# A fused attention and two-layer expert kernel: the region of fixed emission order is taken out and the framework's scheduler orders every engine

## The chip, the cores and the metric

The kernel runs on one core of a Trainium2 chip. The metric is device time in microseconds of one execution, as the median of several runs. A core has five engines that run side by side, each with a queue of its own in a fixed order: TensorE (PE in the profile, with its weight loads shown as PEld), VectorE (DVE), ScalarE (ACT), GpSimd (POOL) and SyncE (SP), which here only issues transfers. Transfers run on 16 DMA engines.

## The reference, cut to what matters

```python
scores = q @ k.T / sqrt(64)              # 4 batches, 8 heads, 576 positions, head size 64
scores = where(block_i >= block_j, scores, -1e9)      # blocks of 64 positions
attn = exp(scores - max); attn /= sum(attn) + 1e-9
x = (attn @ v) as 2304 tokens x 512
x2 = (sigmoid(x @ w_gate) * (x @ w_val)) @ w_out      # 512 -> 1536 -> 512
e = argmax(x2 @ r_gate); p = softmax(x2 @ r_gate)[e]  # one of 8 experts for each token
out = p * (relu(x2 @ w1[e]) @ w2[e])                  # 512 -> 1024 -> 512
```

## The kernel before

All of it is one Python function, `attn_moe_moe_kernel` (L25 to L1322), whose inner functions emit instructions. The body from L1072 on stands in a region of fixed emission order:

```python
    with tc.manual_schedule():          # L1072
        ag = attention()
        ...
        for n, (kind, u, f) in enumerate(msegs):       # L1121: unit u, 128 columns f
            if kind == "g":
                while wdone[0] < count(t_in(f)):
                    next(wg)
                m_gate(u, f)
            elif kind == "v":
                m_val(u, f)
                if f < KF - 1 or not DEFER:
                    m_act(u, f)
```

In such a region every engine issues its instructions in the order in which the Python code emits them. That order is written out by hand, as strings of letters: in `Q0` to `Q4` (L94), `G0` to `H4` (L99) and `TICK0` to `TICK2` (L87, L112), each letter emits one step and a bar separates segments. Semaphores between the engines are the framework's in any case.

The work goes through four stages.

- **Attention of the first batch** (`quick`, L411). A pair is two heads of a batch; an item is 128 query rows of a pair, five items to a pair, 80 in all. An item's steps are S (scores on PE, L253 for the first batch, L262 and L269 later), M (row maximum on DVE, L290 or L292), E (exp on ACT, L306), r and c (reciprocal of the sum on DVE, L323, L325), N (normalizing, L360 on DVE or L358 on ACT), T and U (transposes on PE, L337, copied out by ACT, L339), V (times v on PE, L382) and X (two halves of the result on ACT and DVE, L390, L391, stored by a GpSimd transfer, L393). K and Q (`prep`, L211) transpose the next pair's k and q (L216). Two items are under way at a time.
- **Conversion of the weights** (`weights`, L595). The three matrices of the first layer come as 64-bit numbers, are rounded to 32 bits and split in a high and a low part: two ACT operations (L569, L588) and four DVE operations (L570, L574, L579, L590) for each piece of 128x1024. The letter d and a pacing counter (`pace`) step this generator between the steps of the attention, later between those of the first unit. `w_load` (L550) issues a piece's transfer, 1 MB, into one of four buffers as soon as the code knows that the buffer has been read.
- **The first layer** (units u = 0 to 8 of 256 tokens, 12 column blocks f each). `m_gate` and `m_val` do 12 matmuls each (L633 to L635), `m_act` the sigmoid and the product on ACT and DVE (L654 to L658), `m_out` the second product (L670). The first six units or so are interleaved with the attention of batches 2 to 4: a credit counter calls `seg()`, which emits the attention up to the next bar. In the last unit the routing (`route_early`, small DVE operations) and the first expert's splits (`early_split`) are stepped in between, and `x_trans(0)` (L1007) transposes the first gathered rows behind `m_val` of f = 10.
- **The experts** (`tick`, L1236, 20 slots of 128 tokens). Each slot has `gemm1` and `gemm2` in halves (L1021), `h_trans` and `x_trans` (PE transposes, an ACT copy, and a DVE subtraction, L1044 and L1010), and four splits of the next expert's weights, each an ACT cast (L974) and a DVE subtraction (L975), after which SP loads the weights of the slot after next. `TICK1` is "AxB0amy1CD2b3": A and C are the halves of `gemm1`, B and D those of `gemm2`, a and b the transposes of h, x that of the next slot's rows, 0 to 3 the splits.

Buffers are few: the scores have one PSUM buffer in the later stages, transposes and attention outputs share two (`ea`), gate and value products two (`gv`), exp results two, k and q one each.

Of the kernel before, what the change touches and what calls it, by code (L numbers as in the profile page):

```python
# [24 lines left out]
def attn_moe_moe_kernel(  # L25
# [1043 lines left out]
        )  # L1069


    with tc.manual_schedule():  # L1072
        ag = attention()
        done = [-3]

# [277 lines left out]
```

## Time and profile before

| what | value |
|---|---|
| median of 3 runs | 1022.13 us (1018.63 to 1022.52) |
| the profiled execution | 1020.07 us, of which 1018.3 us lie between the first and the last instruction |
| busy: PE, DVE, ACT, POOL | 945.5, 619.3, 588.0, 122.6 us |
| mean granted clock of PE | 0.986 |

Busy times are read as sums over the whole span: matmuls overlap one another, so PE at 100% of a stretch may still have no more than its instructions in a row. A row of stretches gives, for each stretch, the busy time of each engine, the granted clock as a share of full speed, the mean share of the DMA engines and the rate in GB/s.

### The profile page before, as it was taken

To read this page: it belongs to the slowest core of one execution; us is meant where nothing else is said; L and a number is where in the kernel's file an instruction comes from. 1 tells how busy PE (TensorE), PEld (TensorE's weight loads), DVE (VectorE), ACT (ScalarE), POOL (GpSimd) and SP (SyncE) were. 2 spreads that over 40 slices of the span, in tenths; PEclk is the share of its full clock that TensorE was granted. 3 is DMA by queue.
4 is the path that set the end of the run, shared out by engine and by line. 5 is a ranking of instruction groups with operands and counts; after the bars stand their busy time and mean duration, and the time that the engine had idled before them with its cause. 6 is when DMAs were issued, how large, how long until landed. Compare 5 with 4: busy or idle time off the path is not lost. (4 is left out here: it accounts for less than half of the span.)

```text
span 1018.3 us, 17756 instructions
## 1 busy us (share of the span) xinstructions
PE 945.5 (93%) x6636; PEld 809.0 (79%) x6636; DVE 619.3 (61%) x1178; ACT 588.0 (58%) x1204; POOL 122.6 (12%) x169
## 2 busy tenths in 40 slices
PE   6767887999999999999999999999979999999994
PEld 3444776888888888988888889999968888888883
DVE  5997876545445445445444321122749999888985
ACT  5877555655544554555545321212358878888884
POOL 1111000111001000010010100000022223112110
PEclk9898999999999999999999999999999999999998
DMA  9965240511221131131130110101551552969110
GB/s 253 278 191 178 72 120 26 138 44 41 76 65 41 56 84 36 58 82 42 46 81 14 46 41 1 63 1 63 189 169 57 209 170 82 375 228 340 47 42 20
DMA packets 111161, 106.07 MB, mean 104 GB/s; under 512 B 62175, under 2 KB 83679, under 8 KB 111072
## 3 DMA queue, kind: packets, MB, share of 16 engines
q1 hardware_dynamic: 104128, 84.97, 27.1%
q0 software_dynamic: 6944, 19.93, 5.9%
q8 instruction: 54, 0.88, 0.4%
q14 instruction: 35, 0.29, 0.1%
HBM read 140.53 MB, written 19.40 MB: 157 GB/s over the span
## 5 line engine op out<-in xcount | busy, mean ns | idle before, releaser
L633 PE MATMUL gv<-xu,w 128*128 128x256 f32 x864 | 253.5, 293 | 0.8 <-ACT et L339 0.8
L635 PE MATMUL gv<-xu,w 128*128 128x256 f32 x864 | 244.3, 283 | 1.6 <-DVE w L590 1.6
L634 PE MATMUL gv<-xu,w 128*128 128x256 f32 x864 | 244.2, 283 | 0.0
L975 DVE TENSOR_TENSOR el<-raw,eh 128x2048 fp32r<-128x2048 f32 x84 | 191.7, 2290 | 27.0 <-ACT eh L974 25.8
L670 PE MATMUL acc<-w,g 128*128 128x512 f32 x648 | 184.1, 410 | 3.9 <-ACT g L657 3.9
L633 PEld LDWEIGHTS gv<-xu,w 128*128 128x128 f32 x864 | 165.0, 191 | 7.7 <-issue 5.0
L634 PEld LDWEIGHTS gv<-xu,w 128*128 128x128 f32 x864 | 165.1, 191 | 1.5
L635 PEld LDWEIGHTS gv<-xu,w 128*128 128x128 f32 x864 | 164.7, 191 | 1.8 <-DVE w L590 1.8
L974 ACT CAST eh<-raw 128x2048 fp32r<-128x2048 f32 x84 | 161.0, 1918 | 5.2 <-DMA raw<-in_moe_w_dram 5.1
L655 DVE SCALAR_TENSOR_TENSOR th<-th,gv 128x256 f32<-128x256 f32 x108 | 45.4, 420 | 150.6 <-ACT th L654 150.5
L670 PEld LDWEIGHTS acc<-w,g 128*128 128x128 f32 x648 | 111.5, 190 | 24.2 <-ACT g L657 4.3
L654 ACT ACTIVATE th<-gv 128x256 f32<-128x256 f32 x108 | 41.5, 385 | 133.7 <-PE gv L635 133.5
L393 POOL DMA_DIRECT2D x_d<-x x80 | 55.0, 688 | 494.2 <-DVE x L391 289.8
L1021 PE MATMUL hp<-eh,xt 128*128 128x512 f32 x320 | 109.2, 402 | 0.0
L1021 PE MATMUL yp<-eh,ht 128*128 128x512 f32 x320 | 106.2, 393 | 0.7 <-ACT ht L1043 0.7
L306 ACT ACTIVATE e<-sp,nm 128x128 f32<-128x128 f32 (+3 forms) x128 | 66.5, 526 | 49.9 <-DVE nm L290 47.3
L657 ACT CAST g<-th 128x256 fp32r<-128x256 f32 x108 | 43.9, 406 | 67.5 <-DVE th L655 62.9
L658 DVE TENSOR_TENSOR g<-th,g 128x256 fp32r<-128x256 f32 x108 | 45.9, 425 | 53.3 <-ACT g L657 53.3
L382 PE MATMUL av<-et,v 128*64 128x128 f32 (+1 forms) x960 | 67.7, 273 | 8.0 <-ACT et L339 6.1
L337 PE MATMUL ep<-ident,e 128*128 128x128 f32 x320 | 57.3, 285 | 15.0 <-ACT e L358 5.6
L1021 PEld LDWEIGHTS yp<-eh,ht 128*128 128x128 f32 x320 | 59.9, 188 | 13.6 <-ACT ht L1043 0.9
L1021 PEld LDWEIGHTS hp<-eh,xt 128*128 128x128 f32 x320 | 60.2, 188 | 11.8
(182 smaller groups left out, 1399.6 us busy)
## 6 DMA issues: line engine op xcount, KB each, us to landing
raw<-in_moe_w_dram SPq DMA_DIRECT2D x88, 1024.0 KB
xu<-x_d SPq DMA_DIRECT2D x36, 256.0 KB
x_d<-x POOLq DMA_DIRECT2D x64, 128.0 KB, 2.2
spare<-in_moe_w_gate_dram SPq DMA_DIRECT2D x10, 512.0 KB
spare<-in_moe_w_val_dram SPq DMA_DIRECT2D x10, 512.0 KB
spare<-in_moe_w_out_dram SPq DMA_DIRECT2D x10, 512.0 KB
x_d<-x2r SPq DMA_DIRECT2D x9, 512.0 KB
k<-in_k_dram SPq DMA_DIRECT2D x32, 128.0 KB
```

The source lines that it names most:

```text
L306: nc.scalar.activation(out=r["e"][:, j, 0:n], in_=r["view"][:, j, :], func=AF.Exp, bias=r["nm"][:, j:j + 1], accum_out=su[:, j:j + 1],)
L337: nc.tensor.transpose(ep[:, cs], r["e"][:, part, cs], ident)
L382: nc.tensor.matmul(av[hs, 0:m], lhsT=d["v"][:, c, j, :], rhs=rhs, start=(c == 0), stop=(c == t))
L393: nc.gpsimd.dma_start(out=x_d[hp][:, :, t0:t0 + m], in_=x[:, :, 0:m].bitcast(F32))
L633: nc.tensor.matmul(o, lhsT=wh, rhs=x[:, 0, :], start=(kk == 0 and nm == "g"), stop=False, **kw)
L634: nc.tensor.matmul(o, lhsT=wh, rhs=x[:, 1, :], start=False, stop=False, **kw)
L635: nc.tensor.matmul(o, lhsT=wl, rhs=x[:, 0, :], start=False, stop=(kk == KD - 1), **kw)
L658: nc.vector.tensor_tensor(out=g[:, 1, :], in0=th, in1=g[:, 0, :], op=ALU.subtract)
L670: nc.tensor.matmul(o, lhsT=g[:, part, hs], rhs=w_o(w, f), start=(f == 0 and w == "h" and part == 0), stop=(f == KF - 1 and part == 1),)
L974: nc.scalar.copy(out=h, in_=raw[j])
L975: nc.vector.tensor_tensor(out=l, in0=raw[j], in1=h, op=ALU.subtract)
L1021: nc.tensor.matmul(o, lhsT=t[:, cs], rhs=w[:, c * 512:(c + 1) * 512], start=(first and c == 0 and part == 0 and w is eh), stop=(last and c ...
```

## The change

The region is replaced by an empty context, so the same Python code emits the same instructions with the same buffers in the same sequence, but no engine is held to that sequence.

```diff
@@ -1069,7 +1069,7 @@
         )
 
 
-    with tc.manual_schedule():
+    with ExitStack():
         ag = attention()
         done = [-3]
 
```

The framework then runs its list scheduler when the kernel is built. It walks through the program in a modelled time of its own; whenever an engine is free in it, it takes, among the instructions of that engine whose inputs and buffers are ready by the model, the one emitted first. The outcome is again one fixed order for each engine, which the chip follows as it followed the order by hand.

## Rows read from the trace of the kernel before

**Rows 1.** The page's first lines: span, busy time and instructions of each engine

```profile
span 1018.3 us, 17756 instructions
...
PE 945.5 (93%) x6636; PEld 809.0 (79%) x6636; DVE 619.3 (61%) x1178; ACT 588.0 (58%) x1204; POOL 122.6 (12%) x169
```

**Rows 2.** Busy time in stretches: start:end, length, engines, PE clock, DMA, GB/s

```profile
0.00:25.00 25.00, 16.09 (x82) 8.90 (x82) 14.37 (x32) 14.04 (x35) 2.71 (x10) 1.00 0.94 251
25.00:95.00 70.00, 48.99 (x376) 30.62 (x377) 62.45 (x116) 55.83 (x136) 11.39 (x21) 0.88 0.69 210
95.00:175.00 80.00, 65.77 (x507) 57.94 (x505) 60.20 (x144) 47.66 (x125) 7.27 (x14) 0.98 0.32 93
175.00:225.00 50.00, 48.07 (x383) 41.21 (x384) 27.33 (x74) 27.17 (x80) 5.53 (x12) 1.00 0.31 85
225.00:600.00 375.00, 366.74 (x2953) 326.18 (x2951) 175.77 (x481) 187.95 (x535) 37.36 (x71) 1.00 0.21 56
600.00:740.00 140.00, 140.00 (x1032) 129.18 (x1031) 44.95 (x132) 35.19 (x81) 2.63 (x1) 1.00 0.18 61
740.00:780.00 40.00, 34.68 (x203) 28.82 (x202) 25.02 (x23) 26.82 (x33) 7.77 (x6) 1.00 0.40 126
780.00:1000.00 220.00, 219.76 (x1088) 182.34 (x1087) 202.38 (x178) 188.33 (x179) 46.92 (x36) 1.00 0.50 175
```

**Rows 3.** What PE waited for in 0 to 95 us: total, times, longest

```profile
PE ep L337 <- ACT e L358: 5.6, 5, 1.7
...
PE ep L337 <- DVE e L360: 4.7, 7, 1.0
```

**Rows 4.** DVE's groups in 25 to 95 us: busy us, mean ns, idle before

```profile
L574 DVE SCALAR_TENSOR_TENSOR spare<-spare,spare 128x1024 int32<-128x1024 int32 x10 | 12.2, 1215 | 0.0
L579 DVE CUSTOM_DVE_ANT_0 spare<-spare,spare 128x2048 uint16<-128x2048 uint16 x10 | 12.1, 1213 | 0.0
L590 DVE TENSOR_TENSOR w<-spare,w 128x1024 fp32r<-128x1024 f32 x9 | 11.0, 1218 | 0.0
...
L570 DVE TENSOR_SCALAR spare<-spare 128x1024 int32<-128x1024 int32 x9 | 6.4, 715 | 0.0
L391 DVE TENSOR_TENSOR x<-av,x 128x128 fp32r<-128x128 f32 (+1 forms) x15 | 4.1, 274 | 2.5 <-ACT x L390 2.5
```

**Rows 5.** The order of time in the first 25 us, SP and PE

```profile
9.03 1.17 SPq L186 DMA_DIRECT2D k<-in_k_dram  x2
...
16.63 0.51 SPq L557 DMA_DIRECT2D spare<-in_moe_w_gate_dram  x1
...
19.39 1.12 PE L216 MATMUL tp<-ident,k 128*128 128x128 f32 x5
```

**Rows 6.** One of DVE's groups in 225 to 600 us

```profile
L391 DVE TENSOR_TENSOR x<-av,x 128x128 fp32r<-128x128 f32 (+1 forms) x47 | 12.8, 272 | 25.7 <-ACT x L390 25.5
```

**Rows 7.** What PE waited for in 225 to 600 us: total, times, longest

```profile
PE ep L337 <- ACT et L339: 2.7, 2, 1.4
PE tp L216 <- issue: 2.6, 3, 0.9
PE sp L262 <- ACT x L390: 2.2, 3, 0.8
```

**Rows 8.** The order of time around 742 us, PE

```profile
742.06 0.28 PE L635 MATMUL gv<-xu,w 128*128 128x256 f32 x1
...
745.50 0.66 PE L1007 MATMUL xtp<-ident,xs 128*128 128x128 f32 x4 [3.16 <-DMA xs<-x_d,gi]
...
745.91 0.36 PE L633 MATMUL gv<-xu,w 128*128 128x256 f32 x1
```

**Rows 9.** The order of time in one expert slot, DVE and PE

```profile
857.95 0.69 DVE L1044 TENSOR_TENSOR ht<-htp,ht 128x512 fp32r<-128x512 f32 x1
858.55 2.29 DVE L975 TENSOR_TENSOR el<-raw,eh 128x2048 fp32r<-128x2048 f32 x1
...
859.37 1.07 PE L1021 MATMUL yp<-eh,ht 128*128 128x512 f32 x4
```

## The prediction, made before the changed kernel was run

> **What bounds the kernel now.** I read the page's busy line first. PE is busy for 945.5 of 1018.3 us [rows 1]: it is the engine to look at, and 72.8 us of idle time is all that any order could win from it, because the change adds and removes no instruction.
>
> Then I cut the span into stretches by stage [rows 2], and the reader is to see four regimes. From 0 to 95 us (attention of the first batch, with nine or ten weight pieces converted in between) PE is busy 65.1 of 95 us and DVE 62.5 of the 70 us from 25 on, 89%: DVE is the fullest engine, and PE waits in chains of small steps, most of all for the normalized rows [rows 3]. From 95 to 225 us (first unit, the rest of the conversion) PE lacks 16.2 us while DVE has 19.8 us free from 95 to 175. From 225 to 740 us PE is the bound, idle for 8.3 us of 515. At 740 to 780 us, the passage to the experts, it lacks 5.3 us. From 780 to 1000 us it lacks 0.2 us of 220, but DVE stands at 92% there (202.38 of 220) and ACT at 86%, so the experts are close to a second bound. The last 18 us hold the drain and the end of the program; no order of the work ahead changes them.
>
> So the idle time that could be won is early, and the long stretches that could be lost are full already.
>
> **The change, part by part.** It removes edges of order and nothing else. The scheduler takes the ready instruction that was emitted first. Where the head of the emission order is ready in its model, it repeats the order by hand; it departs from that only where the model says that the head must wait. So each term below is a place where heads wait today, and the trace doesn't show what the model thinks of them: both ends are bounded, and the value is a choice.
>
> *Conversion moved forward, 95 to 225 us.* DVE's 19.8 free microseconds from 95 to 175 [rows 2] hold 4.5 pieces at 4.36 us each (1.215 + 1.213 + 1.218 + 0.715) [rows 4]. If they are used, the first unit's weights come earlier, and PE's 16.2 idle microseconds go at best entirely. At worst nothing is won, since the free time lies in waits on ACT that no piece fits into. I take half: -8 (0 to -16).
>
> *Conversion in front of the attention, 25 to 95 us.* An operation that has begun isn't interrupted. The conversion runs on DVE for 41.7 of the 70 us in 38 operations, 1.10 us each [rows 4]. By hand it stands behind chosen letters; a scheduler that fills every gap starts one whenever the attention's next step is a moment away. An item comes to DVE four times (M, r, N, X); 15 items pass here by the count of L391 [rows 4]. With DVE in a conversion 60% of the time and half an operation, 0.55 us, to wait: 15 x 4 x 0.60 x 0.55 = 19.8 us if nothing covers it, and 0 if the order by hand has paid all of it already, for which PE's 21 idle microseconds there speak. Two items are under way, so I take half: +10 (0 to +20).
>
> *Loads overtaken on SP, 0 to 25 us.* Today SP issues the second pair's k at 9.03 us and the next weight pieces only from 16.63 us on [rows 5]. Pieces two to four have free buffers from the start and may go ahead of k, which waits for its one buffer. Three pieces of 1.05 MB at 251 GB/s [rows 2] are 12.5 us of transfer. Covered is what lies between the issue of k at 9.03 and its use at 19.39 us [rows 5], less its own flight: +2 (0 to +12). SP's later waits are for buffers in either order, and GpSimd, busy for 122.6 us in all [rows 1], has room for its stores: 0.
>
> *Attention between the unit's matmuls, 225 to 600 us.* 48 items pass here (47 in the row's count, where a record may be missing) [rows 6]. PE waited 7.5 us in eight waits, 0.94 us each [rows 7], because a segment of matmuls stands between each producer and PE's next use. The scheduler knows no such margin: it puts the transposes where its model has the rows ready, and a wait appears whenever ACT or DVE is later than modelled. One new wait in every four items gives 12 x 0.94 = +11; one in each item +45; none, and the present ones filled, -8. I take +11, since PE is full and heads are mostly ready.
>
> *Passage to the experts, 740 to 780 us.* PE stands for 3.16 us behind a gathered block while the next unit block's matmuls, which run right after it, wait in line [rows 8]. A scheduler moves these ahead. I take -3 (-5.3, all the idle time, to +2.3, one split of 2.29 us [rows 9] in front of a routing step).
>
> *Splits in the experts, 780 to 1000 us.* In the slot shown, DVE delivers the low half of h at 858.64 (857.95 + 0.69) and PE uses it at 859.37: 0.73 us of margin, and the split right behind takes 2.29 us [rows 9]. If one more split goes in front, PE stands for 2.29 - 0.73 = 1.56 us. There are 20 slots with two such steps. None is lost at best, 40 x 1.56 = 62 us at worst. By the model the low half is ready about when it is today and was emitted before the split, so I take one in ten: 4 x 1.56 = +6.
>
> The sum is -8 + 10 + 2 + 11 - 3 + 6 = +18. The profiled execution took 1020.07 us, 1.8 us over its span of 1018.3 [rows 1]; with +18 it is 1038. It lies 2.1 us under the median of the runs (1022.13), so I forecast 1040 us.
>
> Of the clock: PE's granted clock is 0.88 from 25 to 95 us, a mean of its two levels, 2.4 and 1.2 GHz, and 1.00 where PE is full [rows 2]. The Trainium skill (TensorE: Matmul & The Clock Gate, "What's actually happening") says that the low level is the default and that activity releases it; by that, a fuller PE in this stretch would also run faster. At 0.88 a quarter of PE's 49.0 busy microseconds would be at half speed, about 6 us to win as an estimate from the row. I leave it out of the sum, because DVE and not PE is the fullest there.
>
> **The rivals.**
>
> *The order hardly changes (no difference).* If the heads are ready in the model nearly everywhere, the scheduler repeats the emission order. For it: PE, where all is decided after 225 us, is full, so its heads are ready. Against it: DVE and ACT wait often (DVE 25.5 us in one group alone [rows 6]), so their orders will change. It gives 1022 us, 1017 to 1027.
>
> *The gaps are filled (faster).* The mechanism is the conversion on DVE from 0 to 175 us: it decides if the last piece is converted some 10 us earlier than today with the first batch's attention ending no later than today, about 97 us. Then 12 of the 16.2 idle microseconds go, and 3 at the passage: 1022 - 15 = 1007 us. For it: DVE's free 19.8 us [rows 2]. Against it: DVE is full just before, and the end of the attention depends on steps that wait behind conversions. The Trainium skill (Perfetto Trace Analysis, "Optimization Strategy") says that interleaving regimes with different bounds may improve a kernel; this rival is that rule, and the rows agree that the first 175 us have two regimes.
>
> *The experts and the attention both lose their margins (much slower).* One split in front of one of the two low halves in each slot costs 20 x 1.56 = 31 us, and a wait in every second attention item 24 x 0.94 = 23 us; with +10 and +2 early and no gain: +66, 1088 us. For it: DVE at 92% and a margin of 0.73 us. Against it: the emission order ranks the low half first.
>
> **How the numbers follow.** The forecast's own case (1028 to 1062) has 0.42, much slower 0.20, no difference 0.14, faster 0.24. Half a percent, 5 us, is about what a measurement of this kernel can tell from no change. So slower has 0.62, the same 0.14, faster 0.24. The range goes from 1002, under the faster case, to 1090, over the much slower one; what lies outside is a gain of all the bounds together or a loss near them.
>
> **What would show it.** In the changed profile I would look at the same stretches. Right: PE's first 95 us with more idle time than 29.9 us and the first gate matmul later than now; the last conversion (L590) earlier than now; in 225 to 600 us more and shorter waits of PE on L339 and L360; the gather's wait gone; in the experts waits of PE on L1044. The prediction is wrong if the first 225 us shrink by more than 10 us and the rest stands, or if the experts' stretch grows by tens of microseconds, or if some resource that I have not priced, such as a buffer taken by later work, makes PE stand for long at one place.

## The result, and the profile after

The changed kernel is a little faster: 1018.86 us as the median of 19 runs (1004.75 to 1020.65), against 1023.29 (1018.63 to 1026.48, 19 runs) of the kernel before. The ratio is 0.9912, with a 95% interval of 0.9883 to 0.9941; it is taken from means, without the three runs over 1020 us, which count as slow; with all 19 the means give 0.9922, and the two medians 0.9957. I had forecast 1040 us, slower.

The 19 times lie in two groups, and the groups are those of PE's mean granted clock: nine runs of 1004.75 to 1015.12 us at 0.975 to 0.991, and ten of 1018.86 to 1020.65 us at 0.967 to 0.969. The profile shown here is of a run of the first group: 1009.74 us.

The page's first lines and its row of PE's clock in 40 slices:

```profile
span 1007.8 us, 17820 instructions
...
PE 957.1 (95%) x6636; PEld 811.4 (81%) x6636; DVE 610.5 (61%) x1178; ACT 591.9 (59%) x1204; POOL 127.7 (13%) x169
...
PEclk9997999999999999999999999999999999999998
```

It is the same work as in [rows 1], in a span 10.5 us shorter. The stretches of [rows 2], of the kernel after:

```profile
0.00:25.00 25.00, 11.99 (x46) 6.26 (x46) 12.75 (x26) 9.55 (x24) 1.10 (x8) 1.00 0.84 232
25.00:95.00 70.00, 60.41 (x393) 33.08 (x391) 58.93 (x116) 56.78 (x139) 13.90 (x25) 0.90 0.81 241
95.00:175.00 80.00, 76.13 (x586) 67.13 (x583) 66.97 (x165) 55.23 (x145) 8.15 (x15) 0.96 0.35 97
...
225.00:600.00 375.00, 372.71 (x2992) 331.43 (x2991) 173.65 (x473) 186.63 (x524) 35.33 (x69) 1.00 0.20 54
...
780.00:1000.00 220.00, 209.20 (x1018) 171.60 (x1017) 186.46 (x158) 174.85 (x166) 48.84 (x33) 0.99 0.48 170
```

The first 25 us are emptier than before on PE (16.09 to 11.99), the next 200 fuller [rows 2]. Fixed times no longer mean the same work, though, so I cut both spans again at four events that every run has: the first scores (L253), the first gate matmul (L633), the last second product of the first layer (L670), and the last expert product (L1021). In us:

| stretch | before | after | change |
|---|---|---|---|
| start to the first scores | 8.33 | 15.01 | +6.7 |
| first scores to first gate | 89.16 | 88.46 | -0.7 |
| first gate to last product of the first layer | 658.4 | 635.2 | -23.2 |
| from there to the last expert product | 250.2 | 255.3 | +5.0 |
| from there to the end | 12.2 | 13.9 | +1.7 |

These add up to the -10.5. The gain is in one stretch; three others give back more than half of it. Where in that stretch it lies is seen by windows laid from the first gate on (97.5 us before, 103.5 after), the first two of equal length in both. Before:

```profile
97.50:177.00 79.50, 65.30 (x504) 57.71 (x501) 60.42 (x147) 45.57 (x121) 6.69 (x14) 0.98 0.29 86
177.00:227.50 50.50, 49.34 (x396) 42.48 (x396) 26.04 (x69) 29.11 (x86) 6.18 (x12) 1.00 0.33 89
227.50:585.30 357.80, 349.54 (x2831) 310.03 (x2829) 171.56 (x467) 181.06 (x518) 35.25 (x63) 1.00 0.20 55
585.30:755.90 170.60, 167.44 (x1209) 154.13 (x1210) 53.51 (x152) 45.18 (x100) 7.47 (x11) 1.00 0.22 75
```

After:

```profile
103.50:183.00 79.50, 78.16 (x617) 70.07 (x616) 64.12 (x165) 54.49 (x146) 7.57 (x14) 1.00 0.34 94
183.00:233.50 50.50, 49.77 (x422) 43.21 (x421) 28.58 (x77) 29.59 (x88) 5.35 (x10) 1.00 0.21 50
233.50:569.20 335.70, 333.41 (x2694) 296.27 (x2694) 162.44 (x439) 174.93 (x492) 33.00 (x60) 1.00 0.20 56
569.20:738.70 169.50, 167.71 (x1209) 153.97 (x1210) 53.01 (x152) 46.02 (x99) 6.88 (x11) 1.00 0.23 80
```

In the 79.5 us while the weights are still converted, PE's idle time fell from 14.2 us to 1.3, and it issued 113 matmuls more (617 against 504). In the next 50.5 us it fell from 1.2 us to 0.7, in the rest of the attention's stretch from 8.3 to 2.3, in the last window from 3.2 to 1.8. These are 20.6 of the 23.2 us; the other 2.6 are busy time of PE, whose clock was 0.98 in the first window before and 1.00 after. The conversion's last operation (L590), before and after:

```profile
176.53 0.42 DVE L590 TENSOR_TENSOR w<-wt,w 128x256 fp32r<-128x256 f32 x1
...
156.81 0.43 DVE L590 TENSOR_TENSOR w<-wt,w 128x256 fp32r<-128x256 f32 x1
```

It ends 53.8 us after the first gate, where it had been 79.5. But PE had not waited for weights in the main. Of the 15.4 us of idle time in these first two windows before, 1.6 were a wait for converted weights; most of the others were for steps of the attention and of the unit, which DVE and ACT do too. One of each kind:

```profile
PE acc L670 <- ACT g L657: 3.9, 2, 3.1
...
PE gv L635 <- DVE w L590: 1.6, 1, 1.6
```

What PE waited for afterwards, in 0 to 95 us, for [rows 3]:

```profile
PE tp L216 <- DVE kn L223: 7.5, 1, 7.5
PE ep L337 <- ACT e L358: 4.7, 3, 2.1
PE tp L216 <- DMA k<-in_k_dram: 4.4, 1, 4.4
...
PE ep L337 <- DVE e L360: 0.2, 1, 0.2
```

In 225 to 600 us, for [rows 7], nothing else is left:

```profile
PE tp L216 <- issue: 1.6, 3, 0.5
PE ep L337 <- ACT et L339: 0.6, 2, 0.3
```

And from 740 to 1000 us, where the kernel before had lost 0.9 us in its experts:

```profile
PE yp L1021 <- ACT y L1061: 3.2, 1, 3.2
PE hp L1021 <- ACT xt L1009: 0.8, 1, 0.8
PE yp L1021 <- ACT ht L1043: 0.7, 1, 0.7
PE yp L1021 <- DVE ht L1044: 0.5, 1, 0.5
PE htp L1041 <- ACT h L1032: 0.3, 1, 0.3
```

So the new waits are not where I had looked for them. One wait of 7.5 us stands at the very start; the order of time on ACT, DVE and PE there, after:

```profile
11.78 1.14 ACT L569 ACTIVATE spare<-spare 128x1024 int32<-128x1024 uint32 x1 [5.83 <-DMA spare<-in_moe_w_val_dram]
11.79 0.69 DVE L570 TENSOR_SCALAR spare<-spare 128x1024 int32<-128x1024 int32 x1 [10.53 <-DMA spare<-in_moe_w_val_dram]
12.40 0.75 DVE L223 COPY kn<-tp 128x576 f32<-128x576 f32 x1
...
13.21 1.12 PE L216 MATMUL tp<-ident,q 128*128 128x128 f32 x4 [7.52 <-DVE kn L223]
```

The scheduler put the first conversion on DVE ahead of the copy of the transposed k (L223). On the chip the piece's transfer let it start only at 11.79 us. The copy, whose transposes had run from 4.38 to 5.68 us, stood behind it, and PE's buffer for the q transposes waits for the copy. By hand the copy ran at 5.61 us and these transposes at 6.56.

### The profile page after: what moved, and what is told of

The parts are those of the page before. It is cut to its first block, busy times and chain, and to the rows that moved or that the text cites. A ratio compares the mean times of both kernels' runs of the same rounds, so it can differ in the third digit from the quotient of the medians.

```text
span 1007.8 us, 17820 instructions
## 1 busy us (share of the span) xinstructions
PE 957.1 (95%) x6636; PEld 811.4 (81%) x6636; DVE 610.5 (61%) x1178; ACT 591.9 (59%) x1204; POOL 127.7 (13%) x169
## 5 line engine op out<-in xcount | busy, mean ns | idle before, releaser
L633 PE MATMUL gv<-xu,w 128*128 128x256 f32 x864 | 253.4, 293 | 0.7 <-ACT et L339 0.7
L975 DVE TENSOR_TENSOR el<-raw,eh 128x2048 fp32r<-128x2048 f32 x84 | 191.9, 2288 | 23.2 <-ACT eh L974 21.7
L670 PE MATMUL acc<-w,g 128*128 128x512 f32 x648 | 184.1, 409 | 1.2 <-DVE g L658 1.2
L633 PEld LDWEIGHTS gv<-xu,w 128*128 128x128 f32 x864 | 164.6, 191 | 8.1 <-issue 5.4
L670 PEld LDWEIGHTS acc<-w,g 128*128 128x128 f32 x648 | 110.6, 189 | 21.2 <-issue 3.3
L1021 PE MATMUL yp<-eh,ht 128*128 128x512 f32 x320 | 108.1, 398 | 4.4 <-ACT y L1061 3.2
L1021 PE MATMUL hp<-eh,xt 128*128 128x512 f32 x320 | 109.0, 402 | 0.8 <-ACT xt L1009 0.8
L306 ACT ACTIVATE e<-sp,nm 128x128 f32<-128x128 f32 (+3 forms) x128 | 67.0, 529 | 23.2 <-DVE nm L290 22.4
L1021 PEld LDWEIGHTS yp<-eh,ht 128*128 128x128 f32 x320 | 60.1, 189 | 18.7 <-ACT y L1061 4.1
L339 ACT COPY et<-ep 128x128 f32<-128x128 f32 (+3 forms) x128 | 53.7, 428 | 30.8 <-PE ep L337 29.2
L1021 PEld LDWEIGHTS hp<-eh,xt 128*128 128x128 f32 x320 | 59.9, 188 | 12.8 <-ACT xt L1009 1.3
L382 PEld LDWEIGHTS av<-et,v 128*64 128x64 f32 x960 | 48.1, 139 | 24.0 <-ACT et L339 7.2
```

The costliest lines, as they stand in the source:

```text
L306: nc.scalar.activation(out=r["e"][:, j, 0:n], in_=r["view"][:, j, :], func=AF.Exp, bias=r["nm"][:, j:j + 1], accum_out=su[:, j:j + 1],)
L339: nc.scalar.copy(out=et[:, 0:w], in_=ep[:, 0:w])
L382: nc.tensor.matmul(av[hs, 0:m], lhsT=d["v"][:, c, j, :], rhs=rhs, start=(c == 0), stop=(c == t))
L633: nc.tensor.matmul(o, lhsT=wh, rhs=x[:, 0, :], start=(kk == 0 and nm == "g"), stop=False, **kw)
L670: nc.tensor.matmul(o, lhsT=g[:, part, hs], rhs=w_o(w, f), start=(f == 0 and w == "h" and part == 0), stop=(f == KF - 1 and part == 1),)
L975: nc.vector.tensor_tensor(out=l, in0=raw[j], in1=h, op=ALU.subtract)
```

## The experiments

All of them put `with tc.manual_schedule():` back around parts of the changed kernel; nothing of the computation changes. My theory from the profile above was that the scheduler wins some 23 us between first gate and passage by moving the conversion forward, and loses in the first batch; what Theory 1 and Theory 2 say of each run stands in its expectation. Each ratio is to the kernel before on the same chip, where that kernel's median lay between 1020.77 and 1024.26 us. "Low clock" is the time in the first 130 us at which the trace's record of the clock grants PE 1.2 GHz, added up from windows of one microsecond: 20.5 us before and 20.5 in the profile after.

That record begins late, with its first entry at 20.15 us before and 25.99 us after; ahead of it the windows, those of [rows 2] too, read 1.00. PE's matmuls show that it ran at the low level there: four transposes of 128x128 (L337) took 1.12 us from 23.43 us on in the profile after, and as many took 0.66 from 25.48 us on before, in a stretch that is recorded at 2.4 GHz. So low clock leaves this first stretch out, and where its length differs it is named below.

**The changed kernel once more**, to see how much of a profile repeats (no edit).

> The changed kernel once more, for a profile of an execution of its own. Its 19 times lie in two groups, some 1005 to 1015 us with mean clocks of 0.975 to 0.991 and some 1019 to 1021 us with 0.967 to 0.969. Theory 1 (PE's clock): if the time is near 1019, the extra low clock lies in the first 130 us, and the milestones from there on are later by the same 10 us. Theory 2 (transfers): the clock is then a result, and one long wait on a transfer, longer than in the profile at hand, stands ahead of it. If the time is near 1009, it tells nothing new.

It took 1008.61 us at a clock of 0.984. Low clock 20.5 us, first gate at 102.52 us, 635.2 us from there to the last product of the first layer: the profile repeats.

**First batch by hand.**

```diff
-        while done[0] < NB - 3:
...
+        with tc.manual_schedule():
+            while done[0] < NB - 3:
...
```

> The first batch's attention, with its share of the conversion, keeps the order by hand; units and experts are the scheduler's. Theory 1 (the gain is made from 95 to 225 us, where the conversion and the first unit are packed): 1000 to 1006 us, since the 6 us that the scheduler loses at the start are saved too, the last conversion near 155 us, and the runs lie close together because the first 95 us with their clock are those of before. Theory 2 (the gain is made in the first 95 us, where the scheduler gets more done): 1018 to 1024 us, as before.

1002.21 us (1000.10 to 1003.23), ratio 0.9782 (0.9752 to 0.9811). First gate at 97.13 us, 636.3 us from there to the last product: what the scheduler wins later doesn't need its order of the first batch, and that order costs time. Theory 1 holds by the time; what wins the gain inside its stretch comes below.

**Everything but the first batch by hand.**

```diff
-        for n, (kind, u, f) in enumerate(msegs):
...
+        with tc.manual_schedule():
+            for n, (kind, u, f) in enumerate(msegs):
...
```

> The reverse: the first batch's attention is the scheduler's, units and experts keep the order by hand. Theory 1: 1022 to 1030 us, no gain and the start's loss, with both kinds of runs. Theory 2: 1005 to 1012 us.

1030.59 us (1020.62 to 1037.37, 12 runs), ratio 1.0033 (0.9997 to 1.0068); the stretch after the first gate is back at 661.8 us. No gain is left, as Theory 1 had it; the median lies 0.6 us over its range. The times spread over 17 us, again by the clock: 1020.62 at 0.993, 1034.71 at 0.972.

**Only the first pair's first steps by hand**, so that the copy isn't held up.

```diff
+        with tc.manual_schedule():
+            while done[0] < 0:
+                seg()
         while done[0] < NB - 3:
```

> Only the first steps (the loads, the first transposes, the first two items' scores) keep the order by hand, the rest is the scheduler's. Theory 1 (VectorE stands for 10.5 us at the start behind a conversion whose weights have not landed, and this delays everything by 6 us): 5 to 7 us under the changed kernel run for run, 999 to 1004 us in the group with the high clock. Theory 2 (the first 95 us are bound by transfers, the stall is made up later): within 2 us of the changed kernel.

1017.46 us (1014.47 to 1019.42), ratio 0.9942 (0.9919 to 0.9965). Neither theory: the first scores came at 9.50 us, 5.5 earlier than in the changed kernel, but the first gate at 113.05, 9.6 later. Low clock was 37.5 us instead of 20.5, and the record of the clock begins only at 39.17 us. Ahead of that a window reads 1.00, but eight transposes of 128x128 took 1.97 us in it, which at 2.4 GHz take 1.27 (shown below for another run):

```profile
35.00:36.00 1.00, 1.00 (x8) 0.84 (x7) 0.57 (x5) 0.46 (x2) 0.64 (x1) 1.00 0.00 0
...
35.29 1.97 PE L337 MATMUL ep<-ident,e 128*128 128x128 f32 x8
...
39.18 1.09 PE L382 MATMUL av<-et,v 128*64 128x128 f32 x14
```

With this first stretch counted, PE was busy at 1.2 GHz for 61.5 us between first scores and first gate, against 29.5 in the changed kernel. The 32 us more cost half of themselves, an estimated 16 us, and this part grew by 15.1 with the same idle time of PE (12.5 us in both). So the early start was won and the clock took more than it gave.

**First batch and experts by hand.**

```diff
+        with tc.manual_schedule():
+            while done[0] < NB - 3:
...
+        with tc.manual_schedule():
+            for s in range(NDYN):
+                tick(s)
...
```

> The first batch's attention and the expert slots keep the order by hand; only units and passage are the scheduler's. From the last product of the first layer to the last product of the experts the scheduler took 254.7 to 255.3 us, the order by hand 249.8 to 250.2. Theory 1 (the scheduler's order of the slots loses these 5 us): 996 to 999 us, 5 under the 1002 of the run with only the first batch by hand, with PE full in the experts. Theory 2 (the slots start badly because of the order in the passage): 1001 to 1004 us.

997.21 us (995.37 to 999.61), ratio 0.9756 (0.9728 to 0.9783). From the last product of the first layer to the last expert product ("experts" below) it takes 250.3 us again instead of 255: the 5 us are lost in the slots. Theory 1 holds.

**All by hand but the first two units.**

```diff
+        with ExitStack() as es:
+            for n, (kind, u, f) in enumerate(msegs):
+                if n == first[2]:
+                    es.enter_context(tc.manual_schedule())
...
```

with the first batch by hand as above.

> By hand but for units 0 and 1, in which the conversion ends. Theory 1 (the 23 us between the first gate matmul and the last product of the first layer are won while weights are converted): 999 to 1005 us: 1002, 5 less for experts by hand, up to 6 more for the waits of PE from 225 to 600 us that the order by hand has and the scheduler's not. Theory 2 (they are won evenly over nine units): 1015 to 1020 us.

1003.58 us (1002.76 to 1006.45), ratio 0.9825 (0.9797 to 0.9854). From the first gate to the last product 640.9 us, against 658.4 by hand and 635.2 with the scheduler throughout: 17.5 of the 23 us are won in the two units in which the conversion ends, with every engine free there, the other 5.7 in the later units and the passage. Theory 1 holds. The windows from its first gate show the first part full:

```profile
98.70:178.20 79.50, 78.92 (x618) 70.72 (x617) 63.55 (x161) 53.58 (x143) 9.70 (x19) 0.99 0.38 108
...
228.70:568.00 339.30, 332.99 (x2694) 296.09 (x2693) 160.85 (x438) 171.79 (x491) 33.44 (x60) 1.00 0.20 55
```

**Which engine's order wins it?** First batch by hand, and after it, to the end, only PE ordered by hand in one kernel, only DVE and ACT in the next, all three in the third (SP and GpSimd free):

```diff
+        with tc.manual_schedule(engines={mybir.EngineType.PE}):
+            for n, (kind, u, f) in enumerate(msegs):
...
```

> The first batch by hand; after it TensorE alone keeps the emission order, VectorE, ScalarE, GpSimd and SyncE are the scheduler's. Theory 1 (what counts is that conversions move into VectorE's and ScalarE's gaps, PE need not change): 1002 to 1008 us. Theory 2 (what counts is that PE takes other matmuls when its head waits): 1015 to 1022 us.

> The reverse: the first batch by hand; after it VectorE and ScalarE keep the emission order, TensorE, GpSimd and SyncE are the scheduler's. Theory 1: 1015 to 1024 us. Theory 2: 1002 to 1008 us.

> The first batch by hand; after it TensorE, VectorE and ScalarE keep the emission order, only SyncE and GpSimd, so the order in which transfers are issued, are the scheduler's. With TensorE alone by hand, and with VectorE and ScalarE alone by hand, the kernel took 1010 us, half of the way from 1021 to 1002; in both the transfers were the scheduler's. Theory 1 (the gain needs compute engines on both sides of a wait to be free, each gives a half): 1018 to 1023 us, as before. Theory 2 (earlier transfers gave the half that both have in common): 1008 to 1013 us.

| by hand after the first batch | time, us | ratio | first gate to last product | experts | last conversion after first gate |
|---|---|---|---|---|---|
| PE | 1010.19 (1007.62 to 1011.41) | 0.9885 (0.9856 to 0.9913) | 641.9 | 255.4 | 48.6 |
| DVE, ACT | 1010.67 (1009.86 to 1014.49) | 0.9902 (0.9873 to 0.9932) | 651.8 | 249.3 | 79.5 |
| PE, DVE, ACT | 1021.51 (1019.59 to 1025.42) | 0.9990 (0.9970 to 1.0010) | 660.9 | 252.6 | 80.8 |

Neither theory holds for the first two alone, which win half each by their times; the stretches tell more. With DVE and ACT free the conversion moves forward and 658.4 - 641.9 = 16.5 us are won, but the experts lose their 5. These engines' steps for the attention and the unit are free in that run as well; no run freed the conversion alone. With PE free the conversion stays and 658.4 - 651.8 = 6.6 us are won: PE fills its own waits. The two add up to the 23. The order on SP and GpSimd alone wins nothing, as Theory 1 had it for the third. PE's first window from its first gate, with PE ordered by hand:

```profile
97.90:177.40 79.50, 75.36 (x586) 66.67 (x585) 62.83 (x158) 51.27 (x138) 9.17 (x18) 0.99 0.36 100
```

and with DVE and ACT ordered by hand:

```profile
94.60:174.10 79.50, 71.06 (x513) 61.33 (x512) 61.02 (x149) 46.90 (x126) 7.46 (x15) 0.96 0.33 94
```

Against 504 matmuls before and 617 after, free DVE and ACT bring 586, a free PE 513.

**In the experts, only ACT by hand** (first batch by hand as above). The longest of the new waits is this one, on ACT and PE, after:

```profile
858.99 1.90 ACT L974 CAST eh<-raw 128x2048 fp32r<-128x2048 f32 x1 [0.87 <-DMA raw<-in_moe_w_dram]
860.79 0.58 ACT L1043 CAST ht<-htp 128x512 fp32r<-128x512 f32 x1
861.27 0.59 ACT L1009 CAST xt<-xtp 128x512 fp32r<-128x512 f32 x1
861.75 0.70 ACT L1061 ACTIVATE y<-yp,gw 128x512 f32<-128x512 f32 x1
...
862.50 0.79 PE L1021 MATMUL yp<-eh,ht 128*128 128x512 f32 x1 [3.22 <-ACT y L1061]
```

A cast of the next expert's weights, which itself had waited for its transfer, stands ahead of the three ACT steps that PE needs.

```diff
+        with tc.manual_schedule(engines={mybir.EngineType.Activation}):
+            for s in range(NDYN):
+                tick(s)
...
```

> The first batch by hand; in the expert slots ScalarE alone keeps the emission order; all else is the scheduler's. Theory 1 (the 5 us lost in the slots come from ScalarE, which casts expert weights ahead of the output y and of the rows' copy that TensorE waits for): 996 to 999 us. Theory 2 (they come from the order on TensorE or VectorE): 1000 to 1004 us, as with the first batch alone by hand.

993.76 us (992.53 to 994.45), ratio 0.9718 (0.9686 to 0.9751): the best of all, by medians 25 us under the changed kernel and 16 under its first group. The experts take 247.2 us, 3 fewer than wholly by hand. From 735 us to the end one wait of PE is left:

```profile
PE yp L1021 <- ACT ht L1043: 0.7, 1, 0.7
```

ACT's order was the fault; the order of DVE and PE is better free.

**Only DVE by hand in the first steps.**

```diff
+        with tc.manual_schedule(engines={mybir.EngineType.DVE}):
+            while done[0] < -1:
+                seg()
```

> The changed kernel, but VectorE alone keeps the emission order in the very first steps, so that the copy of the first k stands ahead of the conversion whose weights land late. Theory 1 (that copy is what delays the start): the first q transposes near 6.5 us instead of 13.2, and, at an equal amount of low clock in the first 110 us, 5 to 7 us less than the changed kernel: near 1003 us at a mean clock of 0.984, near 1013 at 0.968. Theory 2 (the first batch is bound elsewhere): equal times at equal clocks.

1012.66 us (1005.56 to 1016.14), ratio 0.9892 (0.9855 to 0.9930): not told apart from the changed kernel. The copy ran at 5.71 us and the q transposes at 7.82, as wanted, but then ACT stood behind its own conversion step:

```profile
10.85 1.12 ACT L569 ACTIVATE spare<-spare 128x1024 int32<-128x1024 uint32 x1 [5.16 <-DMA spare<-in_moe_w_val_dram]
11.86 0.59 ACT L221 ACTIVATE qn<-tp 128x512 f32<-128x512 f32 x1
...
12.50 0.80 PE L253 MATMUL sp<-kn,qn 64*128 64x128 f32 x4 [3.59 <-ACT qn L221]
```

The first scores gained 2.5 us of the 6.7; the second engine's queue has the same head waiting for the same transfer. Low clock was 37.5 us, so this run's end says nothing of the 2.5.

**The changed kernel a third time**, for a profile of the other group.

> The changed kernel a third time, for a profile of an execution of the group near 1019 us, if it falls there. Theory 1 (PE's clock): the low clock in the first 130 us is some 30 us longer than in the profile at hand (20.5 us), and the first gate matmul is about 10 us later. Theory 2 (transfers): a longer wait on a transfer there.

1020.32 us at 0.967. Low clock 58.0 us, 37.5 more than in the profile after; first gate at 116.73 us, 13.3 later; from there to the last product 635.3 us, as ever. The wait at the start is no longer than before (6.8 us, was 7.5). Theory 1, PE's clock, holds. One window of both and the PE rows around it, first of the profile after:

```profile
35.00:55.00 20.00, 18.26 (x127) 10.17 (x125) 18.08 (x36) 17.98 (x46) 4.08 (x7) 0.97 0.68 213
...
32.78 1.97 PE L337 MATMUL ep<-ident,e 128*128 128x128 f32 x8 [2.10 <-ACT e L358]
...
36.24 1.09 PE L382 MATMUL av<-et,v 128*64 128x128 f32 x14
```

and of this run:

```profile
35.00:55.00 20.00, 19.27 (x84) 10.09 (x82) 10.96 (x25) 10.80 (x29) 2.93 (x5) 0.53 0.57 186
...
31.85 1.27 PE L337 MATMUL ep<-ident,e 128*128 128x128 f32 x8 [1.35 <-ACT e L358]
...
35.22 1.97 PE L382 MATMUL av<-et,v 128*64 128x128 f32 x14
```

The same 14 matmuls take 1.09 us at 2.4 GHz and 1.97 at 1.2. In both runs the clock fell after PE had stood for ACT (2.10 and 1.35 us). In one it fell at 32.8 us and was back at 36.2, in the other it fell at 33.4 and stayed low to 53.9 us, although PE was busy for 19.27 of the 20 us shown; only 84 matmuls were issued there where the first run issued 127.

In five kinds of run the first batch is left to the scheduler, wholly or but for its first steps. Between first scores and first gate, with the stretch ahead of the clock's record counted as low:

| profile | length, us | PE idle | PE busy at 1.2 GHz |
|---|---|---|---|
| everything but the first batch by hand | 83.7 | 12.5 | 20.3 |
| the changed kernel | 88.5 | 12.5 | 29.5 |
| the changed kernel a third time | 102.6 | 12.2 | 64.1 |
| only the first steps by hand, DVE alone | 98.0 | 14.1 | 46.1 |
| only the first steps by hand, all engines | 103.5 | 12.5 | 61.5 |

PE's idle time hardly differs. The length goes with the time at low clock: from the changed kernel's it differs by -4.8, +14.1, +9.5 and +15.1 us, and half of the difference in the last column is -4.6, +17.3, +8.3 and +16.0.

## Why the prediction was wrong, point by point

My sum was +18 and the span changed by -10.5, 28.5 us apart. Two terms make 27.7 of it. *Attention between the unit's matmuls* was +11 and came out at -6.0. *Conversion in front of the attention* was +10, and its part came out at -0.7. The steps that failed there are the two that put a new wait of PE behind the scheduler's reordering: the wait whenever ACT or DVE is later than modelled, and half an operation of waiting at each of an item's four steps on DVE. The others, by PE's idle time or the length of their part: conversion moved forward -13.3 for -8, loads +6.7 for +2, passage -1.4 for -3, experts +5.0 for +6, the end after the last expert product, which I had held fixed, +1.7, and PE's busy time after the first gate, which had no term, -2.6.

*Conversion moved forward: right direction, well over half the size, and the way to it in part open.* I took -8 of -16. PE's idle time fell by 13.3 us in the 130 us after the first gate, the part won 17.5 us where all engines were free in the first two units, and 16.5 where DVE and ACT were free and PE was not. The step that failed is "at worst nothing is won, since the free time lies in waits on ACT that no piece fits into", and halving for it: PE's idle time in the first 79.5 us after the gate went down to 1.3 us. The conversion does end earlier, as I had it; that PE's idle time goes because the weights come earlier is not shown, for only 1.6 us of its waits were for them. The Trainium skill (Perfetto Trace Analysis, "Optimization Strategy"), which I had named beside the rival, says that interleaving regimes with different bounds may improve a kernel; these runs agree in the size of the gain, 16.5 to 17.5 us, and don't show that interleaving alone brought it.

*Conversion in front of the attention: wrong.* I took +10 for four half-operations of waiting in every item. Instead the waits of PE went down: PE's idle time between first scores and first gate was 89.16 - 64.27 = 24.9 us before and 88.46 - 75.92 = 12.5 after, and the wait for the DVE rows that I had looked at went from 4.7 to 0.2 us [rows 3]. This hardly shortened the stretch, because PE's busy time for the same matmuls rose by 11.7 us. The clock explains little of that: PE was busy at 1.2 GHz for 26.8 us of the stretch before and 29.5 after, worth 1.4 us. As ends of matmuls are modelled, the rest stays open. Where the same order met a better clock (everything but the first batch by hand), the stretch took 97.36 - 13.63 = 83.7 us.

*Loads overtaken on SP: wrong mechanism, larger loss.* The premise was misread: by hand, too, weight pieces are issued ahead of the second pair's k (9.03 us [rows 5]), not only from 16.63 us on. Before:

```profile
4.98 0.51 SPq L557 DMA_DIRECT2D spare<-in_moe_w_val_dram  x1
...
7.85 1.07 SPq L557 DMA_DIRECT2D spare<-in_moe_w_out_dram  x2
```

After, SP issues the same loads in the same sequence over the first 22 us, with the second pair's k at 10.14 us, so nothing was overtaken. The loss of 6.7 us came from DVE and ACT, whose next instruction waited for a transfer; that the model had it land earlier is my reading, the trace doesn't show the model. I had named such a resource only in general ("that I have not priced").

*Attention between the unit's matmuls: wrong sign.* +11 forecast; PE's idle time went from 8.3 to 2.3 us, near the -8 that I had given as the best case. The step that failed is "a wait appears whenever ACT or DVE is later than modelled": two waits on L339 were left, of 0.6 us together.

*Passage: right in kind, half the size.* -3 forecast. The gather's wait of 3.16 us [rows 8] is down to 0.6; the idle time of the last stretch before the experts fell by 1.4.

*Splits in the experts: the size right by luck, the engine wrong.* +6 forecast, +5.0 measured. PE's waits on DVE's low half (L1044) are 0.5 us; the loss is ACT's casts ahead of y and xt, and ACT's order alone by hand removes it.

*The clock: left out of the sum, which was the second error.* I had seen 6 us to win in it and dropped them because DVE is the fullest there. Nothing was won, and what the clock costs is not fixed: 20.5 us at low clock in one run and 58.0 in another of the same program, whose first gate came 13.3 us later. That is what makes the measured ratio 0.9912 and not the 0.987 of the first group's median (1009.68 over 1023.29).

The rival "the gaps are filled" had its first condition met, the last piece 19.7 us earlier, and gave 1007 us, against 1009.68 at the better clock; that they lie so close is in part luck. Its second condition, an attention that ends by 97 us, wasn't met (first gate at 103.47); it won because the freer orders of DVE and ACT and PE's own filling were worth 23 us, not the 15 that I gave it. My chance of 0.62 for slower rested on margins that the order by hand was supposed to hold; in the units it held waits.

## What to carry to other kernels

A scheduler's order and one by hand need not be chosen for the whole kernel: cut the span at events that every version has, and keep the better order for each stage and engine. Here that is the hand's for the first batch (all engines) and for ACT in the experts, the scheduler's elsewhere: 993.76 us, where neither whole order is under 1004. Where the scheduler lost, an engine that does work for two stages had the head of its queue waiting for a transfer while the other stage's step behind it was ready: look there first, at the start above all, and at every engine of the chain, since freeing one showed the same head on the next.

## What the runs showed of the hardware that was not expected

The granted clock of the same program differs from run to run, and by enough to hide or feign a change of one per cent. After a wait of PE of one to two microseconds the clock fell near 33 us in two runs; it came back after 3.4 us in one and after 20.5 in the other, although PE was busy for 19.27 of 20 us there. The Trainium skill (TensorE: Matmul & The Clock Gate, "What's actually happening") says that activity releases the low level; in this run it was not released for these 20 us.

PE also starts at the low level, and the trace's record of the clock leaves that out. With the first batch by hand the record begins, and PE's matmuls become short, at 20.2 to 21.4 us (the kernel before and seven here); by the scheduler at 24.7 to 26.6, and at 39.2 where only the first steps of all engines were by hand. A mean clock that is taken over the whole span counts this stretch as full speed.

How far the times spread goes in part with the order of the first batch. With that order by hand, the times of a kernel lay within 1.9 to 5.8 us of one another in seven kernels here (5 to 12 runs each) and within 7.5 to 9.8 for the kernel before (four series of 11 to 19 runs); by the scheduler, within 15.9 us (the changed kernel, 19 runs) and 16.8 (everything but the first batch by hand, 12 runs), with 5.0 and 10.6 (8 and 6 runs) where only first steps were by hand. What in the order decides it stays open: no run added work to PE to hold its clock.
